# A three-part edit around float64 weights: the test for tiny values, the place of the rounding, and one normalisation step

## Chip, core and metric

The kernel runs on one core of one Trainium2 chip. The metric is the device time of one execution in microseconds (us); less is better. A core has a matrix engine (TensorE, PE in the profile, with its weight loads as PEld), a vector engine (VectorE, DVE), an activation engine (ScalarE, ACT), a general engine (GpSimd, POOL) and a queue engine (SyncE, SP) that issues the DMAs. Each engine works off its own instructions in a fixed order and waits on semaphores for the others.

## What is computed

```python
# 1. gated linear attention, B=4, H=8, S=768, D=48
state = f[t] * state + outer(k[t], v[t]);  y[t] = q[t] @ state
# 2. gated mixing branch (d_ff = 1024)
h = relu(x @ w_in);  u, v = h[..., :512], h[..., 512:]
v_n = (v - mean(v)) / sqrt(var(v) + 1e-6)
v_s = einsum('ts,bsd->btd', w_spatial, v_n) + b_spatial[None, :, None]
x = (u * v_s) @ w_out
# 3. token and channel layers (d_tok = 256, d_ch = 1536)
h = relu(x.T @ w_tok1) @ w_tok2;  u = x + h.T
out = u + relu(u @ w_ch1) @ w_ch2
```

Six weights (`w_in`, `w_out`, `w_t1`, `w_t2`, `w_c1`, `w_c2`) arrive as float64 and are read as pairs of 32-bit words; `w_sp` is float32.

## The kernel before, in words

The program is unrolled Python. A planner (the tile framework, with a time estimate of its own) sets each engine's order: it goes by the program's order where several instructions could go, and lets a later one go ahead when its data and its buffer are there. What the text writes as a place in the program is therefore a rank and not a time.

All float32 products are made of three products of rounded halves: a tile is split into a high part (`h`, fp32r) and a low part (`l`), and `mm3` (L158 to L164) issues high·high (L162), high·low (L163) and low·high (L164).

**Rounding of a weight piece.** `rounded` (L58 to L80) takes one piece of 128 rows by at most 384 columns: SP loads the raw words into `wst` (three buffers), DVE builds the exponent and sign (L66, L69), ACT scales the low word (L73), POOL adds the two (L74), ACT squares the high word (L75), and DVE (L79) sets to zero what is tiny, by comparing that square with `LEAST`. The result is in `wsa` (three buffers). `split_weight` (L101 on) makes the halves of a piece at once; `round_weight` (L82 on) stores rounded pieces in DRAM for later. There are 47 pieces: 9 of `w_in` and 4 of `w_out` go through `split_weight`, and 6 of `w_t1`, 4 of `w_t2`, 12 of `w_c1` and 12 of `w_c2` (the list `early`) through `round_weight`. `staged` runs a list of pieces as a pipeline of up to five steps, and `weave` spreads such lists evenly among the steps of a main list.

**Order of the stages.** Attention of the first half of batch 0 beside the pieces of `w_in`; then for each batch `s1` (two halves: `norm`, which is L424 to L445, makes v and its normalisation, `gate` makes u) and `s23` (`mix`: the product with `w_sp`, and `out1`: the product with `w_out`), with the attention of the next batch woven in. `norm` ends with L440 on DVE (`vf`, subtract the mean and multiply by `rs`), L444 on ACT (`vh`) and L445 on DVE (`vl`). The list `early` is woven in by `part`, in fifths: the mixing of batch 0, then `s1` of the second half and the mixing of batches 1 and 2. Then come the token layer (`c1`, `c2`) and the channel layer (`ff`), which runs over 4 batches by 2 halves by 12 blocks: `up1` is 9 matmuls into `p`, ACT makes `hh` (L641), DVE makes `hl` (L642), and `down` is 9 matmuls into three sums `po` (L654). For the next batch `c1` loads `xf` (L573) and ACT splits it (L576).

**The flag.** After the first pass `flag` says whether a decay product in `pend` was under `LOW`; if so, `body(True)` computes all again by a slower way. L550 to L556 make the flag. With the inputs here the second pass doesn't run.

Of the kernel before, what the change touches and what calls it, by code (L numbers as in the profile page):

```python
# [18 lines left out]
def tile_kernel(ctx, tc, fkqs, v, w_in, w_sp, b_sp, w_out, w_t1, w_t2, w_c1, w_c2, out):  # L19
    nc = tc.nc  # L20
# [34 lines left out]

    LEAST = 3.4332275390625e-05 ** 2

    def rounded(stage, a, src, c0, width, name):  # L58

# [14 lines left out]
        nc.gpsimd.tensor_tensor(out=a, in0=a, in1=lo, op=ALU.add)  # L74
        nc.scalar.activation(f32(hi), f32(hi), AF.Square)  # L75
        yield

        a = f32(a)
        nc.vector.scalar_tensor_tensor(out=a, in0=f32(hi), scalar=LEAST, in1=a, op0=ALU.is_ge, op1=ALU.mult)  # L79
        return a  # L80

    def round_weight(stage, src, name):  # L82

        if src.dtype != mybir.dt.uint64:
            return src, []
        rows, cols = src.shape
        dst = dram.tile([rows, cols], F32, name=name + "d")
        srcr = src.bitcast(U32).rearrange("(n p) c -> n p c", p=P)

        def piece(i, c0, width):  # L90
            at = stage.tile([P, WST], U32, tag="wsa", name=f"{name}da{i}{c0}")
            a = yield from rounded(stage, at[:, :width], srcr[i], c0, width, f"{name}d{i}{c0}")
# [8 lines left out]
    def split_weight(pool, stage, src, name, n, cols, eng, first=0, order=None, psum=None):  # L101

# [7 lines left out]
        def piece(i, c0, width):  # L110
# [3 lines left out]
            if wide:  # L114
                a = yield from rounded(stage, a, srcr[first + i], c0, width, f"{name}{i}{c0}")
                nc.scalar.copy(h[sl], a)
# [49 lines left out]
    def body(general):  # L166
# [248 lines left out]
        def s1(b, hf):  # L415
# [8 lines left out]
            def norm(i):  # L424
# [31 lines left out]
        def s23(b):  # L456
# [41 lines left out]
        winh, winl, steps = split_weight(  # L498
            wr, wst, w_in, "win", NK, DFF, nc.tensor, order=lambda x: sorted(x, key=lambda y: -y[1]), psum=ps_m
        )  # L500
# [3 lines left out]
        wsph, wspl, st_a = split_weight(wl, wst, w_sp, "wsp", NCH, S, nc.tensor, psum=ps_m)  # L504
        wouth, woutl, st_b = split_weight(wl, wst, w_out, "wout", NJ, DM, nc.tensor, psum=ps_m)
        s10, a01, sa = s1(0, 0), att(half(0, 1)), staged(st_a)
# [4 lines left out]
        early = []  # L511
        if not general:
            for name, src in (("wt1", w_t1), ("wt2", w_t2), ("wc1", w_c1), ("wc2", w_c2)):
                kept[name], x = round_weight(wst, src, name)
                early += x
            early = staged(early)
# [30 lines left out]

        if not general:
# [141 lines left out]
        op = e(tc.tile_pool(name="op", bufs=2))  # L690
        otp = e(tc.tile_pool(name="otp", bufs=3))
        c2h, c2l, st_c = split_weight(w3p, wst, kept["wc2"], "wc2", NF, DM, nc.vector)
# [68 lines left out]
```

## Time and profile before

| | |
|---|---|
| Time, median of 3 runs | 821.85 us (820.16 to 822.72) |
| The profiled execution | 819.0 us, of which its span (first to last instruction) is 817.2 us |
| PE busy | 777.3 us, 95% of the span |
| DVE, ACT, POOL busy | 420.3, 289.1, 211.1 us |
| Mean granted TensorE clock | 0.978 of full speed |
| DMA | 73.74 MB moved, 28% of the 16 engines' span |

How to read the rows further down: a row of a group of instructions gives line, engine, operation, what it writes and reads, the shapes, the count, then busy us and the mean ns of one, then the idle time before them and what ended it. A row of the chain of waits gives the shares of a stretch in the chain that ended last, by engine and line. PE's busy time is modelled from pipelined matmuls, so a PE that is busy all the time may still do less work than another.

### The profile page before, as it was taken

How to read it: one execution, taken by the hardware profiler on the slowest of the kernel's cores; microseconds unless marked ns; L12 is line 12 of the kernel's file. 1: busy time of each engine (PE TensorE's matmuls, PEld its weight loads, DVE VectorE, ACT ScalarE, POOL GpSimd, SP SyncE). 2: the span in 40 equal slices, each digit the busy share in tenths (PEclk: the TensorE clock that was granted, in tenths of full speed). 3: DMA queues.
4: the chain of work that ended last, by engine and by line, in shares of the span. 5: the costliest groups of instructions: out<-in, count | busy, mean ns of one | idle time of the engine just before them, and what ended most of it. 6: DMA issues, size and time to landing. Idle time of an engine off the chain costs nothing.

```text
span 817.2 us, 12758 instructions
## 1 busy us (share of the span) xinstructions
PE 777.3 (95%) x4860; PEld 716.3 (88%) x4860; DVE 420.3 (51%) x820; ACT 289.1 (35%) x649; POOL 211.1 (26%) x265
## 2 busy tenths in 40 slices
PE   5899899898989999999999999999999999999996
PEld 3577688688779888899899999999999999999995
DVE  6968599899898846673552532122122212221211
ACT  5766464555553444231632531122111211221110
POOL 4524344555641212110760330004000400010000
PEclk9899899999999999999999999999999999999998
DMA  7563435766474321220441410002000200000000
GB/s 254 176 207 104 147 96 164 236 225 214 146 237 140 101 96 59 65 67 24 128 126 40 138 56 30 1 4 85 1 30 0 87 1 30 1 8 24 30 1 33
DMA packets 39847, 73.74 MB, mean 90 GB/s; under 512 B 5216, under 2 KB 29664, under 8 KB 39776
## 3 DMA queue, kind: packets, MB, share of 16 engines
q1 hardware_dynamic: 39776, 72.83, 27.7%
q8 instruction: 40, 0.66, 0.3%
q14 instruction: 31, 0.25, 0.1%
HBM read 54.72 MB, written 15.73 MB: 86 GB/s over the span
## 4 chain that ended last, share of the span: by engine, by line
PE 71%; DVE 10%; DMA 10%; issue 4%; ACT 2%; SPq 1%; POOL 1%; DVEq 0%; ACTq 0%; POOLq 0%
PE po L654 19%; PE p L164 8%; PE p L162 8%; PE p L163 8%; DMA fkq<-in_fkq 3%; PE ps L162 3%; PE ps L164 3%; PE ps L163 3%; PE pa L259 2%; PE py L309 2%; PE py L315 2%; PE px L162 2%; PE px L163 1%; PE px L164 1%; DVE pg L236 1%
## 5 line engine op out<-in xcount | busy, mean ns | idle before, releaser
L642 DVE SCALAR_TENSOR_TENSOR hl<-p,hh 128x384 fp32r<-128x384 f32 x96 | 53.3, 557 | 188.4 <-ACT hh L641 188.4
L641 ACT ACTIVATE hh<-p 128x384 fp32r<-128x384 f32 x96 | 47.2, 492 | 198.0 <-PE p L164 198.0
L654 PE MATMUL po<-hl,wc2h 128*128 128x384 f32 x288 | 97.3, 338 | 0.0
L654 PE MATMUL po<-hh,wc2l 128*128 128x384 f32 x288 | 96.7, 336 | 0.0
L665 POOL TENSOR_TENSOR us<-uh,ul 128x384 f32<-128x384 f32 x24 | 24.3, 1024 | 232.0 <-DVE ul L625 214.7
L654 PE MATMUL po<-hh,wc2h 128*128 128x384 f32 x288 | 75.0, 336 | 0.0
L162 PE MATMUL ps<-wsph,vh 128*128 128x384 f32 x192 | 67.5, 351 | 0.0
L163 PE MATMUL ps<-wspl,vh 128*128 128x384 f32 x192 | 66.4, 346 | 0.0
L164 PE MATMUL ps<-wsph,vl 128*128 128x384 f32 x192 | 66.1, 346 | 0.0
L164 PE MATMUL p<-uh,wc1l 128*128 128x384 f32 x192 | 65.0, 338 | 0.0
L264 POOL TENSOR_SCALAR_AFFINE_SELECT am<-am 128x384 f32<-128x384 f32 x64 | 46.9, 748 | 69.7 <-ACT am L263 69.5
L163 PE MATMUL p<-ul,wc1h 128*128 128x384 f32 x192 | 64.7, 337 | 0.0
L162 PE MATMUL p<-uh,wc1h 128*128 128x384 f32 x192 | 64.2, 338 | 0.0
L654 PEld LDWEIGHTS po<-hl,wc2h 128*128 128x128 f32 x288 | 54.1, 188 | 0.1
L654 PEld LDWEIGHTS po<-hh,wc2l 128*128 128x128 f32 x288 | 54.1, 188 | 0.0
L654 PEld LDWEIGHTS po<-hh,wc2h 128*128 128x128 f32 x288 | 52.3, 188 | 0.0
L236 DVE TENSOR_TENSOR_SCAN pg<-fs,first 128x384 f32<-128x384 f32 x32 | 33.3, 1039 | 22.2 <-ACT first L379 22.1
L259 PE MATMUL pa<-fkq 48*128 48x128 f32 x384 | 40.6, 316 | 3.0 <-ACT am L263 3.0
L259 PEld LDWEIGHTS pa<-fkq 48*128 48x128 f32 x384 | 30.5, 204 | 12.3 <-issue 4.3
L162 PEld LDWEIGHTS ps<-wsph,vh 128*128 128x128 f32 x192 | 37.1, 193 | 2.4 <-issue 1.6
L625 DVE TENSOR_TENSOR ul<-p,uh 128x384 fp32r<-128x384 f32 x24 | 13.4, 557 | 47.6 <-ACT uh L624 47.6
L163 PEld LDWEIGHTS ps<-wspl,vh 128*128 128x128 f32 x192 | 37.0, 193 | 0.5 <-issue 0.2
(419 smaller groups left out, 1928.5 us busy)
## 6 DMA issues: line engine op xcount, KB each, us to landing
fkq<-in_fkq SPq DMA_DIRECT2D x31, 578.0 KB, 4.5
vt<-in_v SPq DMA_DIRECT2D x8, 576.0 KB, 5.9
x1d<-xs SPq DMA_DIRECT2D x24, 192.0 KB, 2.0
xf<-x1d SPq DMA_DIRECT2D x12, 384.0 KB, 4.5
out<-ot SPq DMA_DIRECT2D x24, 192.0 KB, 2.0
wspsa<-in_w_sp SPq DMA_DIRECT2D x12, 192.0 KB, 2.6
wc1d<-wc1da SPq DMA_DIRECT2D x12, 192.0 KB, 2.4
wc2d<-wc2da SPq DMA_DIRECT2D x12, 192.0 KB, 2.2
```

The lines of the kernel that those rows point to most:

```text
L162: nc.tensor.matmul(ps, lh, rh, start=first and i == 0, stop=False, **kw)
L163: nc.tensor.matmul(ps, lh, rl, start=False, stop=False, **kw)
L164: nc.tensor.matmul(ps, ll, rh, start=False, stop=i == n - 1, **kw)
L236: nc.vector.tensor_tensor_scan(out=pc, data0=fs[:, :W], data1=first, initial=0.0, op0=ALU.mult, op1=ALU.add)
L259: nc.tensor.matmul(pa[j][:, c, :], ki[64 * j : 64 * j + D, sl], qi[64 * j : 64 * j + D, sl], start=True, stop=True)
L264: nc.gpsimd.affine_select(out=am[j], in_=am[j], compare_op=ALU.is_ge, fill=0.0, base=0, pattern=[[0, NCW], [1, C]], channel_multiplier=-1,)
L309: nc.tensor.matmul(py[:112, c, :], now[c][:112, :112], qi[:112, c * C : (c + 1) * C], start=c == 0, stop=False, skip_group_check=True,)
L315: nc.tensor.matmul(py[64 * j : 64 * j + m, c, :], vt[:, c, h0 + D * j : h0 + D * j + m], am[j][:, c, :], start=False, stop=True, skip_grou ...
L641: nc.scalar.activation(hh, ps, AF.Relu)
L642: nc.vector.scalar_tensor_tensor(out=hl, in0=ps, scalar=0.0, in1=f32(hh), op0=ALU.max, op1=ALU.subtract)
L654: nc.tensor.matmul(po[c], l[:, ft, csl], r, start=ft == 0 and x == 0, stop=ft == NF - 1 and x == 2)
L665: nc.gpsimd.tensor_tensor(out=us[c], in0=f32(uh[:, c, tsl]), in1=f32(ul[:, c, tsl]), op=ALU.add)
```

## The change

There are three parts.

1. **The test for tiny values.** In the first pass the square (L75) and the comparison (L79) of all 47 pieces go away; the second pass keeps them. In their place `look` loads the raw words of all 47 pieces once more, during the channel layer of batches 0 to 2 (a pool `lkp` with two buffers), and DVE takes the smallest absolute high word of each row of a piece into a column of `lows`. `judge` scales `lows`, takes it together with `pend` and makes the flag, so a tiny weight now leads to the second pass. It stands in the channel layer of batch 3.
2. **The place of the rounding.** `early` is woven in by fourteenths: none in batch 0, 5 in batch 1 (`s1` of the second half, mixing), 7 in batch 2 (both halves of `s1`, mixing), 2 in `s1` of batch 3. The second pass rounds these weights itself.
3. **The normalisation.** `vf` is made by ACT as `r * rs + mr`, and DVE makes only the 128 by 1 `mr = -mean * rs`.

```diff
-    LEAST = 3.4332275390625e-05 ** 2
+    LEAST = 3.4332275390625e-05
+    NEAR = 3.5e-05
-    def rounded(stage, a, src, c0, width, name):
+    def rounded(stage, a, src, c0, width, name, tiny):
...
-        nc.scalar.activation(f32(hi), f32(hi), AF.Square)
+        if tiny:
+            nc.scalar.activation(f32(hi), f32(hi), AF.Square)
         yield
-        a = f32(a)
-        nc.vector.scalar_tensor_tensor(out=a, in0=f32(hi), scalar=LEAST, in1=a, op0=ALU.is_ge, op1=ALU.mult)
+        a = f32(a)
+        if tiny:
+            nc.vector.scalar_tensor_tensor(
+                out=a, in0=f32(hi), scalar=LEAST**2, in1=a, op0=ALU.is_ge, op1=ALU.mult
+            )
...
+    def look(stage):
+        def piece(n, src, c0, width):
+            st = stage.tile([P, WST, 2], U32, tag="look", name=f"look{n}")
+            nc.sync.dma_start(
+                out=st[:, :width, :].rearrange("p c t -> p (c t)"), in_=src[:, 2 * c0 : 2 * (c0 + width)]
+            )
+            yield
+            nc.vector.tensor_reduce(
+                out=lows[:, n : n + 1], in_=f32(st[:, :width, 1]), op=ALU.min, axis=mybir.AxisListType.X,
+                apply_absolute_value=True,
+            )
...
+                mr = smp.tile([P, 1], F32, tag="mr", name=f"mr{b}{hf}{i}")
                 nc.vector.tensor_scalar(
-                    out=vf, in0=r, scalar1=mv[:, 0:1], scalar2=rs, op0=ALU.subtract, op1=ALU.mult
-                )
+                    out=mr, in0=mv[:, 0:1], scalar1=rs, scalar2=-1.0, op0=ALU.mult, op1=ALU.mult
+                )
+                nc.scalar.activation(vf, r, AF.Identity, bias=mr, scale=rs)
...
-        part = lambda n: early[len(early) * n // 5 : len(early) * (n + 1) // 5]
+        part = lambda n, m: early[len(early) * n // 14 : len(early) * m // 14]
         for b in range(B - 1):
             if b:
-                weave(s1(b, 0), rest)
+                weave(s1(b, 0), rest, part(7 * b - 9, 7 * b - 7) if b > 1 else [])
...
-            weave(a, steps[:cut], out_steps if b == 0 else part(2 * b - 1))
-            weave(m, steps[cut:], part(2 * b))
+            weave(a, steps[:cut], out_steps if b == 0 else part(7 * b - 7, 7 * b - 5))
+            weave(m, steps[cut:], part(7 * b - 5, 7 * b - 2) if b else [])
...
-        weave(rest + s1(B - 1, 0) + s1(B - 1, 1), staged(st_a + st_b))
+        weave(rest + s1(B - 1, 0) + s1(B - 1, 1), staged(st_a + st_b), part(12, 14))
...
+        def judge():
+            nc.vector.tensor_scalar(
+                out=lows[:, :NLOW], in0=lows[:, :NLOW], scalar1=LOW / NEAR, scalar2=None, op0=ALU.mult
+            )
             nc.vector.tensor_reduce(
-                out=least, in_=pend.rearrange("p u c -> p (u c)"), op=ALU.min, axis=mybir.AxisListType.X
+                out=lows[:, NLOW : NLOW + 1], in_=pend.rearrange("p u c -> p (u c)"), op=ALU.min,
+                axis=mybir.AxisListType.X,
             )
+            nc.vector.tensor_reduce(out=least, in_=lows, op=ALU.min, axis=mybir.AxisListType.X)
...
+        looks = [] if general else staged(look(lkp))
+        part = lambda n: looks[len(looks) * n // (2 * B - 3) : len(looks) * (n + 1) // (2 * B - 3)]
         for b in range(B):
...
-                weave(ff(b, 0), ld, st_c[12:] if b == 0 else [])
+                weave(ff(b, 0), ld, st_c[12:] if b == 0 else part(2 * b - 1))
...
-                weave(ff(b, 0))
-            weave(ff(b, 1), more)
+                weave(ff(b, 0), [] if general else [judge])
+            weave(ff(b, 1), more, part(2 * b) if b + 1 < B else [])
```

## Rows read from the trace of the kernel before

**Rows 1.** The page's first part: busy us, share of the span, instructions.

```profile
PE 777.3 (95%) x4860; PEld 716.3 (88%) x4860; DVE 420.3 (51%) x820; ACT 289.1 (35%) x649; POOL 211.1 (26%) x265
```

**Rows 2.** Windows: stretch, length; busy (count) PE, PEld, DVE, ACT, POOL; clock; DMA; GB/s.

```profile
0.00:53.00 53.00, 38.48 (x273) 26.79 (x273) 43.61 (x84) 35.53 (x87) 22.28 (x44) 0.94 0.68 223
53.00:174.00 121.00, 112.01 (x761) 92.41 (x757) 97.79 (x206) 63.64 (x153) 51.95 (x63) 0.94 0.51 162
174.00:281.00 107.00, 100.16 (x679) 87.07 (x678) 95.19 (x190) 51.36 (x120) 45.82 (x54) 0.95 0.54 173
281.00:383.00 102.00, 102.00 (x727) 89.20 (x726) 60.59 (x129) 35.89 (x82) 16.35 (x35) 1.00 0.19 60
383.00:470.00 87.00, 85.62 (x483) 82.82 (x482) 41.55 (x70) 37.42 (x80) 38.74 (x43) 1.00 0.35 106
470.00:809.00 339.00, 339.00 (x1953) 338.05 (x1951) 80.62 (x144) 65.31 (x129) 35.93 (x28) 1.00 0.07 23
```

**Rows 3.** Chain of waits by line, windows 113:174, 174:281, 281:383, 470:817 in turn.

```profile
by line: DMA fkq<-in_fkq 17.1%; issue 12.7%; DMA wt1d30st<-in_w_t 7.2%; DMA wt2d1384st<-in_w_t 6.9%; DMA wc1d01152st<-in_w_c 6.1%; DMA wc1d0384st<-in_w_c 5.5%; DVE fkq L244 4.4%; SPq L93 2.4%; DVE wc1da L66 2.4%; DVE pg L241 2.3%; DVE vl L4
by line: issue 12.8%; PE ps L163 5.1%; PE ps L164 5.0%; DMA wc2d20st<-in_w_c 4.9%; PE ps L162 4.8%; DMA wc1d2768st<-in_w_c 4.5%; DVE wc2da L66 4.2%; DMA wc2d00st<-in_w_c 4.1%; DMA wc2d70st<-in_w_c 3.9%; DVE pg L236 3.6%; DVE wc2da L79 3.4%;
by line: PE ps L162 9.7%; PE ps L164 8.6%; PE pa L259 8.6%; PE ps L163 8.4%; PE py L315 6.2%; PE py L309 6.2%; PE px L162 5.8%; PE pu L162 4.7%; PE px L163 4.6%; PE pv L164 4.5%; PE px L164 4.4%; PE pv L162 4.4%; PE pu L164 4.1%; PE pu L163
by line: PE po L654 43.1%; PE p L164 17.7%; PE p L163 17.6%; PE p L162 17.6%; PE p L614 1.7%; DVE ot L675 0.2%; DVEq L710 0.1%; DVEq L675 0.0%
```

**Rows 4.** Windows of L79's instructions alone (DVE busy, count); then L75's sum.

```profile
0.00:53.00 53.00, 5.21 (x9) 0.94 0.68 223
53.00:174.00 121.00, 11.72 (x20) 0.94 0.51 162
174.00:281.00 107.00, 11.93 (x18) 0.95 0.54 173
...
sum 809.00, ACT 25.33; mean ACT 4.22
```

**Rows 5.** Groups by line: the normalisation, and the nearest operations.

```profile
L440 DVE TENSOR_SCALAR vf<-r,mv,rs 128x512 f32<-128x512 f32 x24 | 18.0, 750 | 9.7 <-POOL rs L438 9.6
L444 ACT CAST vh<-vf 128x512 fp32r<-128x512 f32 x24 | 14.9, 621 | 16.8 <-DVE vf L440 16.7
L576 ACT CAST x1h<-xf 128x768 fp32r<-128x768 f32 x12 | 10.0, 835 | 8.3 <-DMA xf<-x1d 8.1
L434 DVE BATCH_NORM_AGGREGATE mv<-bs 128x2 f32<-128x6 f32 x24 | 4.2, 175 | 0.3
```

**Rows 6.** The last rounding piece in time (start us, us), and the reduction of `pend`.

```profile
243.93 0.35 DVE L66 TENSOR_SCALAR wc2da<-wc2d110st 128x384 uint32<-128x384 uint32 x1
...
L550 DVE TENSOR_REDUCE least<-pend x1: 254/254/254, 360.2 to 360.2; 128x1 f32<-128x96 f32 x1
```

**Rows 7.** DMA issues: count, KB each, median us to landing.

```profile
xf<-x1d SPq DMA_DIRECT2D x12, 384.0 KB, 4.5
...
wout00st<-in_w_out SPq DMA_DIRECT2D x1, 384.0 KB, 3.1
...
wc2d30st<-in_w_c SPq DMA_DIRECT2D x1, 384.0 KB, 5.8
```

**Rows 8.** Waits (us in total, times, longest): ACT in 113:281, then window 470:809.

```profile
ACT wc2d20st L73 <- DMA wc2d20st<-in_w_c: 3.1, 1, 3.1
...
ACT x1h L576 <- DMA xf<-x1d: 6.0, 5, 2.1
```

**Rows 9.** Timeline in `ff`: start us, us, engine, line, what, [idle before].

```profile
487.31 0.49 ACT L641 ACTIVATE hh<-p 128x384 fp32r<-128x384 f32 x1 [2.67 <-PE p L164]
...
487.84 0.56 DVE L642 SCALAR_TENSOR_TENSOR hl<-p,hh 128x384 fp32r<-128x384 f32 x1 [2.61 <-ACT hh L641]
...
488.69 0.35 PE L654 MATMUL po<-hl,wc2h 128*128 128x384 f32 x1
488.87 0.34 PE L654 MATMUL po<-hh,wc2l 128*128 128x384 f32 x1
```

More of the change, by code (lines that the diff above doesn't have):

```diff
@@ L74, in rounded, with round_weight @@
         nc.gpsimd.tensor_tensor(out=a, in0=a, in1=lo, op=ALU.add)
-        nc.scalar.activation(f32(hi), f32(hi), AF.Square)
+        if tiny:
+            nc.scalar.activation(f32(hi), f32(hi), AF.Square)
         yield
         a = f32(a)
-        nc.vector.scalar_tensor_tensor(out=a, in0=f32(hi), scalar=LEAST, in1=a, op0=ALU.is_ge, op1=ALU.mult)
+        if tiny:
+            nc.vector.scalar_tensor_tensor(
+                out=a, in0=f32(hi), scalar=LEAST**2, in1=a, op0=ALU.is_ge, op1=ALU.mult
+            )
         return a
-    def round_weight(stage, src, name):
+    def round_weight(stage, src, name, tiny):
         if src.dtype != mybir.dt.uint64:
@@ L91, in piece @@
             at = stage.tile([P, WST], U32, tag="wsa", name=f"{name}da{i}{c0}")
-            a = yield from rounded(stage, at[:, :width], srcr[i], c0, width, f"{name}d{i}{c0}")
+            a = yield from rounded(stage, at[:, :width], srcr[i], c0, width, f"{name}d{i}{c0}", tiny)
             nc.sync.dma_start(out=dst[i * P : (i + 1) * P, c0 : c0 + width], in_=a)
@@ L99, in tile_kernel, with split_weight @@
     kept = {}
-    def split_weight(pool, stage, src, name, n, cols, eng, first=0, order=None, psum=None):
+    wides = [w for w in (w_in, w_out, w_t1, w_t2, w_c1, w_c2) if w.dtype == mybir.dt.uint64]
+    NLOW = sum(w.shape[0] // P * -(-w.shape[1] // WST) for w in wides)
+    lows = const.tile([P, NLOW + 1], F32, name="lows")
+    def look(stage):
[9 more added lines that the diff above has]
+            )
+        out = []
+        for w in wides:
+            wr = w.bitcast(U32).rearrange("(n p) c -> n p c", p=P)
+            for i in range(w.shape[0] // P):
+                for c0 in range(0, w.shape[1], WST):
+                    out.append(partial(piece, len(out), wr[i], c0, min(WST, w.shape[1] - c0)))
+        assert len(out) == NLOW
+        return out
+    def split_weight(pool, stage, src, name, n, cols, eng, first=0, order=None, psum=None, tiny=False):
         wide = src.dtype == mybir.dt.uint64
@@ L114, in piece @@
             if wide:
-                a = yield from rounded(stage, a, srcr[first + i], c0, width, f"{name}{i}{c0}")
+                a = yield from rounded(stage, a, srcr[first + i], c0, width, f"{name}{i}{c0}", tiny)
                 nc.scalar.copy(h[sl], a)
@@ L498, in body @@
         winh, winl, steps = split_weight(
-            wr, wst, w_in, "win", NK, DFF, nc.tensor, order=lambda x: sorted(x, key=lambda y: -y[1]), psum=ps_m
+            wr, wst, w_in, "win", NK, DFF, nc.tensor, order=lambda x: sorted(x, key=lambda y: -y[1]), psum=ps_m,
+            tiny=general,
         )
@@ L504, in body @@
         wsph, wspl, st_a = split_weight(wl, wst, w_sp, "wsp", NCH, S, nc.tensor, psum=ps_m)
-        wouth, woutl, st_b = split_weight(wl, wst, w_out, "wout", NJ, DM, nc.tensor, psum=ps_m)
+        wouth, woutl, st_b = split_weight(wl, wst, w_out, "wout", NJ, DM, nc.tensor, psum=ps_m, tiny=general)
         s10, a01, sa = s1(0, 0), att(half(0, 1)), staged(st_a)
@@ L511, in body @@
         early = []
[L512 to L516, printed above, removed]
-        part = lambda n: early[len(early) * n // 5 : len(early) * (n + 1) // 5]
+        for name, src in (("wt1", w_t1), ("wt2", w_t2), ("wc1", w_c1), ("wc2", w_c2)):
+            kept[name], x = round_weight(wst, src, f"{name}{int(general)}", general)
+            early += x
+        early = staged(early)
+        part = lambda n, m: early[len(early) * n // 14 : len(early) * m // 14]
         for b in range(B - 1):
             if b:
-                weave(s1(b, 0), rest)
+                weave(s1(b, 0), rest, part(7 * b - 9, 7 * b - 7) if b > 1 else [])
             a, rest = s1(b, 1), []
@@ L546, in body @@
         h1p = wr2.enter_context(tc.tile_pool(name="h1p", bufs=1, side="right"))
-        if not general:
+        def judge():
+            nc.vector.tensor_scalar(
+                out=lows[:, :NLOW], in0=lows[:, :NLOW], scalar1=LOW / NEAR, scalar2=None, op0=ALU.mult
+            )
             nc.vector.tensor_reduce(
-                out=least, in_=pend.rearrange("p u c -> p (u c)"), op=ALU.min, axis=mybir.AxisListType.X
+                out=lows[:, NLOW : NLOW + 1], in_=pend.rearrange("p u c -> p (u c)"), op=ALU.min,
+                axis=mybir.AxisListType.X,
             )
+            nc.vector.tensor_reduce(out=least, in_=lows, op=ALU.min, axis=mybir.AxisListType.X)
             row = ps_s.tile([P, W], F32, tag="s", name="row")[:1, :P]
@@ L691, in body @@
         otp = e(tc.tile_pool(name="otp", bufs=3))
+        lkp = e(tc.tile_pool(name="lkp", bufs=2))
         c2h, c2l, st_c = split_weight(w3p, wst, kept["wc2"], "wc2", NF, DM, nc.vector)
```

## The prediction, made before the changed kernel was run

> **What bounds the kernel now.** First the page's busy line: PE is busy 95% of the span, DVE 51%, ACT 35% [rows 1]. So time can be won only where PE idles or is slowed, and the mean says nothing on where. Next a table by stage [rows 2], with edges where the first normalisation of a batch starts (batch 0 at 53 us, 1 at 174, 2 at 281, 3 at 383; the channel layer from about 470). The reader is to see two halves. From 281 us on PE is busy without a break, but for 1.4 us, and its clock is full: nothing that DVE or ACT save there is worth anything. Before 281 PE idles 14.5, 9.0 and 6.8 us in the three stages, its clock is 0.94 to 0.95, and DVE is busy 82%, 81% and 89%. Then the chain of waits for four stretches [rows 3]: after 281 it is nearly all PE; before, it runs through loads of weight pieces, loads of `fkq` and DVE's steps of the rounding. So the first 281 us are bound by DVE and by the rounding's own chain as much as by PE, and the rest by PE alone.
>
> Stages 174 to 281 and 281 to 383 do the same main work (one batch of `s1` and `s23`, eight attention units), and only the first has rounding: the last of its 47 pieces is begun at 243.9 us [rows 6]. It takes 107 us against 102. The later stage even issues 48 matmuls more (727 against 679) [rows 2]; at the 0.18 us between two matmul starts [rows 9] these are 8.6 us of work. So rounding and the DVE load cost the stage 5 + 8.6, some 13 us, and that is all it can give back.
>
> **Part 1a, L75 and L79 go.** L79 takes 5.2, 11.7 and 11.9 us of DVE in the three stages (9, 20 and 18 pieces), L75 25.3 us of ACT in all [rows 4]. Each piece also loses two steps of its chain, and its `wst` buffer is free earlier, so SP issues the next load sooner.
>
> **Part 3, the normalisation.** DVE loses L440 at 0.75 us and gains a 128 by 1 operation, priced like L434 at 0.175 [rows 5]. This is 0.57 us a time, with 6 in each stage from 53 us on: 3.4 us each. ACT gains `vf`. The trace has no ACT pass with two per-row operands; the bounds are L444, as wide, at 0.62 us, and L576, half as wide again, at 0.84 [rows 5]. I take 0.8, since the two operands must cost something, so 24 x 0.8 = 19 us, less than the 25.3 that L75 frees: ACT ends 6 us lighter. The wait of ACT for DVE, now before `vf` and no longer before `vh`, has the same work queued behind it on ACT (`hh`-like copies, `fs`, `am`), and it ends 0.57 us sooner; then ACT is held 0.8 us longer. In the stages after 281 I cost it at nothing: PE hides it, and if that cover is gone it is 12 x (0.8 + 0.175 - 0.75) = 2.7 us.
>
> **What 1a and 3 give, by stage.** *174 to 281*: DVE falls by 11.9 + 3.4 = 15.3 us, from 95.2 to 79.9, which is 75% of 107. The stage without rounding has 59% (60.6 of 102) [rows 2]. The relief closes 14 of the 30 points, about half, so I take half of the 13 us: **6 us**. Bounds: 0 and 13. *53 to 174*: DVE falls by 11.7 + 3.4 = 15.1 us, from 81% to 68%. What can be won is PE's idle 9.0 us and what the low clock costs: a mean of 0.94 between the levels 0.5 and 1 is 12% of 121 us at half speed, 14.5 us, at most 7.3 us lost; 16 us together. But 17% of the chain there is loads of `fkq` [rows 3], which the change leaves alone; I take a third: **5 us**, bounds 0 and 16. *0 to 53*: the relief is 5.2 us of DVE; the first loads and the chain of the first attention units stay. I take **2 us**, bounds 0 and 5.
>
> **Part 2, the later place.** A place is a rank to the planner, and the trace shows how little it binds: the last piece stands in the mixing of batch 2, after 281 us, and ran at 243.9; the reduction of `pend` stands behind the mixing of batch 3 and ran at 360.2 [rows 6]. The pieces ran ahead of their places as soon as a buffer was free. I expect the same after: every instruction of a piece (its load and its store on SP, L66 and L69 on DVE, L73 on ACT, L74 on POOL) gets a lower rank but is still issued early, on SP ahead of `fkq` loads that stand later, as now. So I take **0**. If the rank does bind, up to 24 of the 38 steps of `early` move behind 281, and the two stages before get DVE, ACT and the DMAs to themselves. That is worth at most what is left of their 13 and 16 us, 18 us; the stages behind have PE full and DVE at 59% and 48% as cover, and without it could lose what 174 to 281 lost before, 13 us. Bounds: -18 and +13.
>
> **Part 1b, the looks.** 47 loads of 384 KB (nine of 256) and 47 DVE reductions come into the channel layer, where PE is full. One reduction is 128 by 384; L550 took 0.25 us for 96 elements and L434 0.175 for 6 [rows 5, 6], so 0.9 ns an element and some 0.51 us, 23 us in all, beside 80.6 us of DVE work in 339 [rows 2]. They will run soon after 470, as fast as two buffers allow, not where they are woven in. The danger is the order on DVE: behind a reduction that waits for its load stands `hl` (L642), and PE's next-but-few matmul waits for that. `hl` ended at 488.40 and was used at 488.69: 0.29 us of slack; DVE idles 2.6 us of each 3.2 [rows 9]. Landed in time, a reduction fits the gap, and a chance overlap costs under (0.51 - 0.29)^2 / 2 / 3.2 us, nothing. Landed late by t, it has 2.6 - 0.5 = 2.1 us of room at most. Loads of this size took 3.1 us (quiet) to 5.8 (busy), `xf` 4.5 [rows 7]; the planner's order was wrong by 1.2 us on the mean for `xf` in this very stage (6.0 us in 5 waits), and by up to 3.1 us for a weight piece [rows 8]. With t = 1.2 and the room spread evenly from 0 to 2.1, a look costs 0.91^2 / 2 / 2.1 = 0.2 us, 47 make 9 us. Those waits are the late ones of 12 `xf` loads, and looks come one at a time, so I take a third: **+3 us**. Bounds: 0 and 47 x (1.2 - 0.29) = 43 us. `out` stores and `xf` loads queue behind looks on SP; the first have the next half to drain, the second are used tens of us later: 0.
>
> `judge` adds two DVE operations of 0.25 us; its one PE transpose waits for them, at most 0.8 us once, and it ends half a batch before the end: 0, in the rounding of the above.
>
> **The sum.** -2 - 5 - 6 + 3 = -10 us against the profiled execution's 819.0, of which 817.2 is the span and 1.8 lies around it. The median of the runs is 821.85, 2.85 above that one; I put the change on the median: **812 us**.
>
> **The rivals.**
> *The looks hold DVE* (ends slower). Two buffers in flight make a loop: load, reduction, next load. If on the chip that loop is slower than in the planner's estimate, DVE's order makes `hl` go at the loop's pace, and each look costs PE the difference. For: the 0.29 us of slack, the waits for `xf`. Against: the DMA share there is 0.07, and a lone load took 3.1 us. At half of the upper bound, 21 us, less the 13 us won before: 830 us. It decides from 13 / 47 = 0.28 us of PE per look on. The Trainium skill ("Perfetto Trace Analysis", section "Tensor Engine Instruction (MATMUL, LD_WEIGHTS)") states that DVE, unlike PE's weight loads, takes its queue strictly in order; the waits of ACT for `xf` in front of `hh` look the same, and it would be this rival's 830.
> *DVE was not what held PE* (no change). Then weight loads, 17% of the chain in 174 to 281 (wc2d20, wc1d2768, wc2d00, wc2d70) [rows 3], still set the pace; the gain shrinks to 3 us and the looks take it back: 822 us.
> *The rank binds*: of the 13 and 16 us most is won, say 22 in place of 11: 801 us.
> *ACT becomes the bound of the normalisation.* All 24 chains get longer by 0.8 + 0.175 - 0.75 = 0.225 us; on the path throughout that is 5 us: 817 us. For: ACT waited 16.7 us for L440 [rows 5]. Against: ACT is busy 48% from 174 to 281 [rows 2]. The Trainium skill ("ScalarE: Activation LUTs", section "Rules for kernel authors") says that adds and multiplies belong on VectorE, which would speak against part 3 and give this 817; its section "What ACT_TABLE_LOAD costs" prices the pass at 0.80 us (an estimate: 186 ns + 0.833 ns x 512 + 93 ns for each per-row operand), which leaves the sum at 812.
>
> **How the numbers follow.** Forecast 0.50, looks hold DVE 0.18, no change 0.15, rank binds 0.12, ACT 0.05. About 0.3% (2.5 us, 819.4 to 824.3) is what a measurement of this kernel can tell from no change. The forecast, with its own range of 805 to 820, is faster in nine tenths of its cases (0.45); with the rank (0.12), ACT (0.04) and a few of the looks' cases (0.02) faster gets 0.63. No change (0.11) and edges of the others give same 0.17, slower 0.20. The range leaves out a tenth at either end: below, half of the rank's cases and the best of the forecast, 798; above, half of the looks' cases, 830.
>
> **What would show it.** *Right*: the stage of batch 1 (174 to 281 now) shorter by about 6 us with DVE near 75%, that of batch 0 by 5; L66 of the pieces still between 70 and 240 us; PE without a break in the channel layer, and DVE's waits for the looks' loads small. *Wrong*: DVE waiting for `look` loads by tens of us with `hl` late behind it, PE idle after 470; pieces spread to 400 us (part 2 was undervalued); DVE far below 75% before 281 with PE's idle time unchanged (DVE was not the bound); ACT idle in front of `vf`, with `vh` and the mixing late.

## The result, and the profile after

The changed kernel takes 831.3 us (median of 4 runs, 828.9 to 835.5) against 821.0 us for the kernel before in the same comparison: 1.0142 times as long, with a 95% interval of 1.0107 to 1.0177. It is slower by 1.4%, where 812 us, faster, was predicted; 831.3 also lies above the range. The rival "the looks hold DVE" had put 830 us.

Where did the time go? I cut both profiled executions at the same points of the work: the first matmul of each batch's `pv` (the product that makes v), the first transpose of `c2`, the first and last `po` matmul, and the matmuls at a quarter and at half of `po`. All lengths are in us.

| stretch | before | after | difference |
|---|---|---|---|
| start, to `pv` of batch 0 | 53.2 | 52.9 | -0.3 |
| batch 0 | 121.0 | 121.0 | 0.0 |
| batch 1 | 106.5 | 101.5 | -5.0 |
| batch 2 | 102.5 | 102.8 | +0.3 |
| batch 3 and `c1`, to the first transpose of `c2` | 70.3 | 70.1 | -0.2 |
| `c2`, to the first `po` | 13.0 | 16.9 | +3.9 |
| channel layer, first quarter | 90.8 | 109.1 | +18.3 |
| channel layer, second quarter | 90.4 | 90.0 | -0.4 |
| channel layer, second half | 161.0 | 160.4 | -0.6 |
| from the last `po` to the end | 8.5 | 6.8 | -1.7 |
| span | 817.2 | 831.5 | +14.3 |

So 5 us were won in batch 1 and 22 us lost in one place, from `c2` to the end of the first quarter of the channel layer. The changed file's lines have moved; the ones that matter here are the look's load (L114) and reduction (L118), `mr` (L472), `vf` on ACT (L475), `hh` and `hl` (L679, L680) and `po` (L692).

The page's busy line of the changed kernel:

```profile
PE 783.2 (94%) x4860; PEld 713.4 (86%) x4860; DVE 409.4 (49%) x822; ACT 285.3 (34%) x626; POOL 206.4 (25%) x265
```

DVE and ACT got lighter, as meant (420.3 and 289.1 us before, [rows 1]), and yet the span grew. So the sums say nothing; the stages do. These are the windows of the changed kernel by stage, with the columns of [rows 2]:

```profile
53.00:174.00 121.00, 112.30 (x757) 91.05 (x758) 91.41 (x191) 59.84 (x139) 52.97 (x66) 0.97 0.56 174
174.00:275.00 101.00, 96.87 (x673) 83.28 (x672) 75.75 (x160) 46.35 (x105) 35.96 (x50) 0.98 0.51 162
275.00:378.00 103.00, 103.00 (x729) 90.61 (x728) 56.78 (x129) 40.21 (x88) 17.15 (x35) 1.00 0.19 60
378.00:465.00 87.00, 82.66 (x462) 79.33 (x460) 39.58 (x69) 38.61 (x80) 40.76 (x43) 1.00 0.40 122
465.00:560.00 95.00, 83.72 (x441) 78.24 (x442) 44.38 (x84) 18.73 (x39) 10.82 (x8) 0.96 0.65 189
560.00:823.00 263.00, 263.00 (x1523) 262.38 (x1522) 60.58 (x112) 49.59 (x98) 25.77 (x21) 1.00 0.07 23
```

The second row is what was hoped for: DVE at 75.75 of 101 us, PE idle 4 us. The fifth is the loss: PE idle 11.3 us, a granted clock of 0.96 and 441 matmuls, in a stretch that was full before. The sixth is full again. DVE is busy only 47% of the fifth stretch, so it isn't short of time; it waits, and the chain of waits from 470 to 560 us names for what:

```profile
by line: DMA look<-in_w_c 48.1%; DMA look<-in_w_t 15.9%; DVE lows L118 11.5%; DMA look<-in_w_in 8.0%; PE po L692 3.6%; DMA look<-in_w_out 3.5%; DVE wc2l L157 2.8%; issue 2.7%; PE p L193 1.5%; PE p L194 1.5%; PE p L195 1.4%; DVE hl L680 1.0%
```

Three quarters are loads of looks and 11.5% their reductions. The timeline shows one turn of the loop (start us, us, engine, line, what, idle before it and for what):

```profile
499.87 0.49 ACT L679 ACTIVATE hh<-p 128x384 fp32r<-128x384 f32 x1 [3.10 <-PE p L195]
...
502.86 0.55 DVE L118 TENSOR_REDUCE lows<-look 128x1 f32<-128x384 f32 x1 [0.97 <-DMA look<-in_w_t]
...
505.01 0.55 DVE L118 TENSOR_REDUCE lows<-look 128x1 f32<-128x384 f32 x1 [1.60 <-DMA look<-in_w_c]
505.48 0.55 DVE L680 SCALAR_TENSOR_TENSOR hl<-p,hh 128x384 fp32r<-128x384 f32 x1
506.08 0.19 PEld L692 LDWEIGHTS po<-hl,wc2h 128*128 128x128 f32 x1 [1.05 <-DVE hl L680]
506.09 0.45 PE L692 MATMUL po<-hl,wc2h 128*128 128x384 f32 x1 [0.73 <-DVE hl L680]
```

Which `hh` belongs to which `hl`, and which `hl` to which matmul? The text's `step(n)` issues `up1` of block n and then `down` of block n-1, and each trace has 96 `hh`, 96 `hl` and 96 groups of three `po<-hl` matmuls, so they are matched by counting. The `hl` of 505.48 belongs to the `hh` that ended at 500.36 and could have started then. But two reductions of looks stood ahead of it on DVE and waited 0.97 and 1.60 us for their loads; `hl` came at 505.48, and PE stood still for 0.73 us. The Trainium skill ("Perfetto Trace Analysis", section "Tensor Engine Instruction (MATMUL, LD_WEIGHTS)") states that DVE takes its queue strictly in order; the trace agrees, since DVE was idle for both of these waits while `hl` was ready.

How early did PE have `hl` before the change? The prediction read 0.29 us, from the `hl` that ended at 488.40 to the matmul at 488.69 [rows 9]. By the count that matmul reads the `hl` of the block before, and the one of 488.40 is used only from 491.68 on. The kernel before:

```profile
484.67 0.56 DVE L642 SCALAR_TENSOR_TENSOR hl<-p,hh 128x384 fp32r<-128x384 f32 x1 [2.61 <-ACT hh L641]
...
491.68 0.19 PEld L654 LDWEIGHTS po<-hl,wc2h 128*128 128x128 f32 x1
```

So `hl` led its user by 3.28 us, a whole block. In blocks 7 to 24, which make up most of the first quarter, the lead was never under 3.07 us before; in the changed kernel it was 0.05 us in 12 of these 18 blocks, with PE waiting, and 3 us again when the looks were over.

The waits from 465 to 560 us (us in total, times, longest) and the group of the reductions over the whole span:

```profile
DVE lows L118 <- DMA look<-in_w_c: 30.1, 24, 2.2
DVE lows L118 <- DMA look<-in_w_t: 10.4, 10, 1.6
PEld po L692 <- DVE hl L680: 13.0, 13, 2.1
PE po L692 <- DVE hl L680: 8.7, 10, 1.8
...
L118 DVE TENSOR_REDUCE lows<-look 128x1 f32<-128x384 f32 (+1 forms) x47 | 24.7, 526 | 50.6 <-DMA look<-in_w_c 30.1 <-DMA look<-in_w_t 10.4 <-DMA look<-in_w_in 7.4
```

DVE waited 50.6 us for 47 loads, 1.08 us each, and PE waited 8.7 us for `hl`, where it waited 0.0 us in the kernel before.

### The profile page after: what moved, and what is told of

It reads as the page before. It is cut to its first block, busy times and chain, and to the rows that moved or that the text cites. A ratio compares the mean times of both kernels' runs of the same rounds, so it can differ in the third digit from the quotient of the medians.

```text
span 831.5 us, 12770 instructions
## 1 busy us (share of the span) xinstructions
PE 783.2 (94%) x4860; PEld 713.4 (86%) x4860; DVE 409.4 (49%) x822; ACT 285.3 (34%) x626; POOL 206.4 (25%) x265
## 4 chain that ended last, share of the span: by engine, by line
PE 56%; DMA 17%; DVE 5%; POOL 2%; SPq 2%; issue 1%; ACT 1%; DVEq 0%; POOLq 0%; ACTq 0%
PE po L692 15%; PE p L195 6%; PE p L194 6%; PE p L193 6%; DMA look<-in_w_c 5%; PE ps L193 3%; PE ps L195 3%; PE ps L194 3%; DMA look<-in_w_in 3%; PE pa L290 2%; DMA look<-in_w_t 2%; PE px L193 1%; DVE lows L118 1%; PE px L195 1%; PE px L194 1%
## 5 line engine op out<-in xcount | busy, mean ns | idle before, releaser
L680 DVE SCALAR_TENSOR_TENSOR hl<-p,hh 128x384 fp32r<-128x384 f32 x96 | 53.2, 555 | 158.5 <-ACT hh L679 158.4
L679 ACT ACTIVATE hh<-p 128x384 fp32r<-128x384 f32 x96 | 47.1, 492 | 198.6 <-PE p L195 198.6
L692 PE MATMUL po<-hl,wc2h 128*128 128x384 f32 x288 | 99.1, 344 | 8.7 <-DVE hl L680 8.7
L692 PE MATMUL po<-hh,wc2l 128*128 128x384 f32 x288 | 97.9, 340 | 0.0
L692 PE MATMUL po<-hh,wc2h 128*128 128x384 f32 x288 | 76.9, 343 | 4.0 <-ACT hh L679 2.5
L692 PEld LDWEIGHTS po<-hl,wc2h 128*128 128x128 f32 x288 | 54.6, 190 | 13.1 <-DVE hl L680 13.0
L295 POOL TENSOR_SCALAR_AFFINE_SELECT am<-am 128x384 f32<-128x384 f32 x64 | 40.1, 636 | 97.0 <-ACT am L294 96.9
L692 PEld LDWEIGHTS po<-hh,wc2h 128*128 128x128 f32 x288 | 53.3, 190 | 5.1 <-ACT hh L679 4.3
L692 PEld LDWEIGHTS po<-hh,wc2l 128*128 128x128 f32 x288 | 54.8, 190 | 0.0
L118 DVE TENSOR_REDUCE lows<-look 128x1 f32<-128x384 f32 (+1 forms) x47 | 24.7, 526 | 50.6 <-DMA look<-in_w_c 30.1
L267 DVE TENSOR_TENSOR_SCAN pg<-fs,first 128x384 f32<-128x384 f32 x32 | 31.5, 985 | 36.2 <-ACT first L410 36.2
L290 PE MATMUL pa<-fkq 48*128 48x128 f32 x384 | 43.8, 313 | 0.0
L290 PEld LDWEIGHTS pa<-fkq 48*128 48x128 f32 x384 | 32.2, 200 | 11.3 <-issue 6.1
L340 PE MATMUL py<-fkq,state 112*112 112x128 f32 x160 | 33.1, 299 | 6.0 <-DVE state L315 3.8
```

The costliest lines, as they stand in the source:

```text
L118: nc.vector.tensor_reduce(out=lows[:, n : n + 1], in_=f32(st[:, :width, 1]), op=ALU.min, axis=mybir.AxisListType.X, apply_absolute_value=True,
L267: nc.vector.tensor_tensor_scan(out=pc, data0=fs[:, :W], data1=first, initial=0.0, op0=ALU.mult, op1=ALU.add)
L290: nc.tensor.matmul(pa[j][:, c, :], ki[64 * j : 64 * j + D, sl], qi[64 * j : 64 * j + D, sl], start=True, stop=True)
L295: nc.gpsimd.affine_select(out=am[j], in_=am[j], compare_op=ALU.is_ge, fill=0.0, base=0, pattern=[[0, NCW], [1, C]], channel_multiplier=-1,)
L340: nc.tensor.matmul(py[:112, c, :], now[c][:112, :112], qi[:112, c * C : (c + 1) * C], start=c == 0, stop=False, skip_group_check=True,)
L679: nc.scalar.activation(hh, ps, AF.Relu)
```

## The experiments

The theory: the looks run early and as a closed loop of two buffers (load, reduction, next load). The planner had put them in DVE's order at the pace that it reckons for this loop; on the chip the loop is slower, and since `hl` stands in between, PE goes at the loop's pace once the lead of `hl` is used up. That the loop is closed is seen in the trace: from the 12th look on each reduction begins 0.02 us after its load has landed, and the load that takes over its buffer is issued 0.03 us after its end. The pace planned can be read from PE: between the reductions at 502.86 and 553.63 us there are 24 looks and 220 matmuls. At 0.173 us a matmul (549 in 94.7 us where PE is undisturbed) these are 38.0 us of work, 1.58 us a look; they took 50.77 us, 2.12 us a look. The excess is 0.53 us a look, 12.8 us in this stretch, in 9.1 of which PE was idle; its granted clock there was 0.97. Rivals: the traffic of the loads slows what else moves; the reductions' own time on DVE is too much; the loss has nothing to do with the looks.

**No looks.** The changed kernel without loads and reductions; `lows` is filled with ones, so tiny weights are not tested for.

```diff
-        looks = [] if general else staged(look(lkp))
+        looks = []
+        if not general:
+            nc.gpsimd.memset(lows, 1.0)
```

> The changed kernel without the 47 looks (their loads and reductions are left out, the column block that they fill is set to 1.0; so the test for tiny weights isn't made). All theories that blame the looks: the channel layer runs at PE's pace as before, about 17 us come back, 812 to 816 us. If the looks are not the cause (a change of order before 465 us is), it stays at 828 to 832 us.

Measured: 813.8 us, 0.9917 of before (0.9884 to 0.9950); first quarter of the channel layer 90.4 us, `c2` 13.0. By the ratios (1.0142 and 0.9917) the looks cost 18 us, and by the cuts of the profiles 22, all of it in that place; the rest of the change is worth -6.8 us.

**Loads only.** The 47 loads stay, the reductions go.

```diff
-            nc.vector.tensor_reduce(
-                out=lows[:, n : n + 1], in_=f32(st[:, :width, 1]), op=ALU.min, axis=mybir.AxisListType.X,
-                apply_absolute_value=True,
-            )
...
+        if not general:
+            nc.gpsimd.memset(lows, 1.0)
```

> The 47 loads stay, nothing reads them (the reductions are left out). Loop theory (DVE stands before a reduction whose load is late, with hl behind it): no wait on DVE, so as without looks, 812 to 817 us. Theory of DMA traffic (17 MB more slow PE, stores or other loads): 826 to 832 us. Theory of DVE's own time: 812 to 817 us.

Measured: 815.8 us, 0.9949 (0.9917 to 0.9980); first quarter 91.3 us, but `c2` 15.3, so 2 of the 4 us lost in `c2` may be the loads' own. Beyond that the traffic is not the cause: the window from 465 to 560 us moves even more per second (197 GB/s) and PE is full.

```profile
465.00:560.00 95.00, 94.73 (x549) 94.18 (x548) 26.43 (x44) 22.91 (x44) 17.74 (x13) 1.00 0.65 197
```

**Reductions only.** One tile stays resident, filled with ones by POOL; the 47 reductions read it, and there are no loads.

```diff
-            st = stage.tile([P, WST, 2], U32, tag="look", name=f"look{n}")
-            nc.sync.dma_start(
-                out=st[:, :width, :].rearrange("p c t -> p (c t)"), in_=src[:, 2 * c0 : 2 * (c0 + width)]
-            )
+            if n == 0:
+                kept["look"] = st = stage.tile([P, WST, 2], U32, tag="look", name="look")
+                nc.gpsimd.memset(f32(st.rearrange("p c t -> p (c t)")), 1.0)
+            st = kept["look"]
```

> The 47 reductions stay, all of one tile that is filled once, with no load to wait for (the loads are left out). Loop theory: 25 us of DVE work fit beside hl, 812 to 818 us. Theory of DVE's own time (a reduction in front of hl uses up its slack of 0.29 us): 824 to 832 us. DMA theory: 812 to 817 us.

Measured: 830.9 us, 1.0120 (1.0073 to 1.0168): the loop theory's expectation missed. But the loss lies elsewhere: `c2` took 22.5 us instead of 13.0 and the first quarter 97.0. Without loads nothing held the reductions back, and the planner put all of them into one stretch, 457 to 486 us, in runs of up to 14, ahead of `wc2l` and `ul`, which the transition to the channel layer needs. The chain of waits from 448 to 500 us says so:

```profile
by line: DVE lows L118 22.3%; PE po L692 17.1%; PE p L195 10.2%; PE p L194 10.1%; PE p L193 9.7%; DMA xf<-x1d 6.6%; DVE wc2l L157 5.5%; issue 3.3%; PE px L195 2.7%; DVE ul L663 2.7%; PE px L193 2.3%; PE px L194 2.3%; PE p L652 2.3%; ACT x1h
```

No load of a look is in it. So this run has a cause of its own, or DVE's time is the cause in both. The run after "paced" below was made to tell these apart.

**Paced.** Loads and reductions as in the change, but each reduction may go on DVE only behind the `hl` that the text puts before it, so that the looks are spread over the half batches in which they are written.

```diff
-            nc.vector.tensor_reduce(
+            with tc.issue_after(kept["hl"].ins):
+                nc.vector.tensor_reduce(
...
-                nc.vector.scalar_tensor_tensor(
+                kept["hl"] = nc.vector.scalar_tensor_tensor(
```

> All 47 loads and reductions, but each reduction is queued on DVE behind the hl that stands before it in the program, so that the looks spread over batches 0 to 2 and a load has about two blocks of the channel layer (some 6 us) to land. Loop theory: the load has landed when DVE comes to its reduction, 812 to 818 us, faster than the kernel before. DVE's own time or DMA traffic: 824 to 832 us as before, since both amounts are unchanged.

Measured: 816.9 us, 0.9952 of before (0.9927 to 0.9976); `c2` 13.1, first quarter 91.8, second 90.1. The same loads, reductions and buffers, without the loss. DVE's waits for looks from 465 to 650 us are now two, of 0.8 and 0.5 us:

```profile
DVE lows L119 <- DMA look<-in_w_c: 0.8, 1, 0.8
...
DVE lows L119 <- DMA look<-in_w_out: 0.5, 1, 0.5
```

**Reductions in the channel layer.** As "reductions only", but held behind the first `hl`.

```diff
+            with tc.issue_after(kept["hl"].ins):
+                nc.vector.tensor_reduce(
...
+                kept["hl"] = kept["hl"] or x
```

> The changed kernel without the 47 loads; 47 reductions of one resident tile, queued on DVE behind the first low part of the channel layer, so that none stands in the stage before it. It tells what made the reductions without loads lose 16 us. If it was the burst in front of the work that the second token layer and the first blocks need: 0 to 2 us lost, 813 to 817 us, the second token layer back at 13 us and the first quarter of the channel layer at 91. If DVE's time behind the slack of the low part is itself the cause: about 0.3 us of PE for each reduction, 825 to 830 us, with the first quarter of the channel layer at 100 us or more.

Measured: 818.6 us, 1.0003 (0.9971 to 1.0035); `c2` 13.0, first quarter 94.3. Between the two expectations, nearer to the burst: 3.5 us are left of the 15.7 that "reductions only" lost in `c2` and the first quarter. And these 3.5 us aren't DVE's time behind `hl`. The windows of the two stretches in which the 47 reductions stand (464 to 492 us):

```profile
464.00:476.00 12.00, 10.11 (x47) 9.53 (x47) 12.00 (x27) 6.28 (x12) 7.94 (x5) 0.86 0.55 172
476.00:494.00 18.00, 18.00 (x105) 18.00 (x105) 17.22 (x38) 3.36 (x7) 0.00 (x0) 1.00 0.00 1
```

All the loss is in the first, where the reductions stand among `wc2l` and `ul` and PE's waits are for the halves of `xf`; what makes these late there is not shown. In the second DVE is busy 96% of the time, and PE has no break. So the reductions' time costs PE nothing where the order leaves `hl` its lead. Against the run without looks the ratio to before is higher by 0.0086, 7 us; each of the two ratios is known to some 3 us, so how much more than 3.5 us is real stays open.

**Four buffers.** The changed kernel with four buffers for the looks.

```diff
-        lkp = e(tc.tile_pool(name="lkp", bufs=2))
+        lkp = e(tc.tile_pool(name="lkp", bufs=4))
```

> The changed kernel with four buffers in place of two for the looks. Loop theory: with four loads under way both the planner's loop and the chip's are bound by the DMAs' rate; a lone load moves 384 KB in about 1.5 us of transfer, so the chip's pace drops from 2.1 to about 1.6 us a look, while the planner crowds them closer as well; if the planner's pace falls in step the loss stays near 17 us (828 to 833 us), if the loop's latency was all, it falls under 8 us (816 to 822 us). Theory of DVE's own time: unchanged, 828 to 833 us.

Measured: 814.3 us, 0.9971 (0.9936 to 1.0005); first quarter 92.9 us. Better than both expectations. The looks run as early as in the change (their reductions from 455 to 518 us), and 2 us are lost in the first quarter: PE waited for `hl` once, 2.0 us, at the first block. From 471.90 to 517.70 us there are 37 looks, one each 1.24 us, and PE has no break, so the PE work between two is as long: no excess. The lead of `hl` is never under 0.59 us after the first block.

```profile
471.90:517.70 45.80, 45.80 (x264) 45.76 (x264) 29.32 (x60) 9.31 (x19) 1.79 (x1) 1.00 0.91 308
```

DVE's waits for looks in all fell from 50.6 to 17.7 us.

**One buffer.** The same with `bufs=1`.

> The changed kernel with one buffer for the looks in place of two: a load is issued only when the reduction of the look before it has ended. Loop theory (the loads' and reductions' loop takes longer on the chip than the planner reckons, and DVE's fixed order hands the difference to the high and low parts and so to PE): the loop is then a whole latency longer and so is the difference, from some 0.5 us a look to about 1.0 us, so 40 to 50 us are lost in the channel layer against 18 to 22, and the time is 850 to 860 us. DVE's time alone as the cause: the same 47 reductions, so the time stays near 831 us. Traffic of the loads as the cause: fewer loads at a time, so the same or less than 831 us.

Measured: 837.3 us, 1.0239 (1.0181 to 1.0296). The direction is the loop theory's, and DVE's time as the cause falls, for the reductions are the same; but the loss is 26 us (`c2` +2.0, first quarter +17.7, second +5.9), not 40 to 50. From 478.65 to 555.39 us there are 22 looks:

```profile
478.65:555.39 76.74, 67.85 (x368) 63.76 (x367) 23.31 (x49) 10.75 (x22) 3.04 (x3) 0.98 0.37 109
```

3.49 us a look, and 368 x 0.173 / 22 = 2.89 us of PE work between two: 0.60 us excess, against 0.53 with two buffers. My expectation took the excess to double, since with two buffers two loads share it. They don't: a load alone in flight lands sooner. The loads of `in_w_c` in the changed kernel, with one buffer and with four (count, KB each, median us to landing):

```profile
look<-in_w_c SPq DMA_DIRECT2D x24, 384.0 KB, 3.5
```

```profile
look<-in_w_c SPq DMA_DIRECT2D x24, 384.0 KB, 3.1
```

```profile
look<-in_w_c SPq DMA_DIRECT2D x24, 384.0 KB, 4.3
```

So more buffers make each load slower and the loop faster. By (load + reduction) / buffers, with 0.55 us for the reduction, a turn is 3.65, 2.03 and 1.21 us with one, two and four buffers; measured were 3.49 (where a third of the looks move only 256 KB), 2.12 and 1.24. Also to be seen: with one buffer DVE waits 102 us for looks, twice as long as with two, and PE loses about as much. Most of that wait was in the plan (2.89 us of PE work to a look) and lay beside other work:

```profile
DVE hl L680 <- ACT hh L679: 117.8, 58, 5.4
DVE lows L118 <- DMA look<-in_w_c: 58.5, 24, 3.2
...
DVE lows L118 <- DMA look<-in_w_t: 23.0, 10, 3.0
DVE lows L118 <- DMA look<-in_w_in: 10.3, 7, 3.3
DVE lows L118 <- DMA look<-in_w_out: 10.3, 4, 2.7
```

**Paced, four buffers.** Both edits together.

> The changed kernel with each look's reduction held behind the low part that the text puts before it, and four buffers for the looks in place of two. Loop theory: the looks, held to their places, leave their loads enough time already with two buffers, so no gain from four: 815 to 817 us, as with two. If waits of DVE for loads still cost something there: 812 to 814 us.

Measured: 817.4 us, 0.9969 (0.9938 to 0.9999); first quarter 91.1 us (`c2` 15.0). No gain over either alone: once the excess is gone, a second cure buys nothing.

**The other parts alone**, each put into the kernel before. First the test taken out (lines L75 and L79) with nothing in its place, so tiny weights are not handled:

```diff
-        nc.scalar.activation(f32(hi), f32(hi), AF.Square)
...
-        nc.vector.scalar_tensor_tensor(out=a, in0=f32(hi), scalar=LEAST, in1=a, op0=ALU.is_ge, op1=ALU.mult)
```

> The kernel before without L75 and L79 (the test for tiny weights is left out), all else as before. By the prediction's stage sums the relief of DVE and the shorter chain of a piece give 2 + 4 + 4.5 us, so 810 to 813 us. Rival: the changed kernel won only 5 us before the channel layer, all of it in the stage of batch 1; then this gives 815 to 819 us, and the stage of batch 0 (53 to 174 us) stays at 121 us because more pieces move into it.

Measured: 818.3 us, 0.9982 (0.9947 to 1.0018): not told from no change, and not the 810 to 813 us of the prediction's sums. In its profile batch 1 was shorter, 102.7 us, and so was batch 0, 115.7 us, which the rival kept at 121; but the start was longer, 57.0 us, so that the first 174.3 us of the kernel before became 172.7.

Then the normalisation alone (its diff stands in the change above):

> The kernel before with vf made on ScalarE and nothing else. By the prediction's sums DVE loses 3.4 us in each of two stages that it holds up: 1 to 3 us won, 818 to 820 us. Rival (the normalisation's chain gets longer by 0.225 us, 24 times, on the path): 2 to 5 us lost, 823 to 827 us.

Measured: 815.6 us, 0.9953 (0.9927 to 0.9978), some 3.9 us faster, a little more than the 1 to 3 expected; batch 1 104.2 us. `vf` on ACT takes 814 ns:

```profile
L444 ACT ACTIVATE vf<-r,mr,rs 128x512 f32<-128x512 f32 x24 | 19.4, 814 | 9.0 <-DVE mr L441 8.6
```

Then the later place alone (the `part` lines of the change):

> The kernel before with the list of later weights woven in by fourteenths from batch 1 on, and nothing else. Rank theory (a place is a rank; pieces run as soon as a buffer is free): L66 of the pieces still between 70 and 250 us but for the last few, time within 3 us of the kernel before. Rival (the place binds): pieces up to 400 us, stages of batch 0 and 1 shorter by up to 18 us together.

Measured: 819.0 us, 1.0003 (0.9979 to 1.0027): nothing. All but two of the pieces were begun by 242.0 us, as before; the last two, which the text puts in batch 3, went at 390.3 and 397.8 us.

Last, the paced kernel with the earlier places:

```diff
-        part = lambda n, m: early[len(early) * n // 14 : len(early) * m // 14]
+        part = lambda n: early[len(early) * n // 5 : len(early) * (n + 1) // 5]
```

> The changed kernel with the looks held as before, and the rounding of the later weights put back at its earlier places. By the run of the later place alone (no change) it should be the same as with the later place, 815 to 818 us. If the later place moves pieces into the stage of batch 0 and so eats up there what the test's leaving gives: the stage of batch 0 falls from 121 to 116 us, that of batch 1 is longer by less, and the time is 812 to 815 us.

Measured: 817.1 us, 0.9977 (0.9951 to 1.0003), batch 0 121.0 us. The place is worth nothing beside the other parts either, and it isn't what kept batch 0 at 121 us: 24 pieces were begun in it with either place.

## Why the prediction was wrong

The step that failed is **Part 1b, the looks**. It had the place (a late load in front of `hl`) and the early start right, and the cost of a look wrong: +3 us for all, where `c2` and the first quarter lost 22. It reckoned the looks as single late events against a slack of `hl`; the runs showed a closed loop that is 0.53 us a turn slower than the order allows for. "Paced", "four buffers" and "loads only" each take away one link of the loop, and each brings the first quarter back to 91 to 93 us.

- *"0.29 us of slack"* was misread: the lead of `hl` was 3.28 us. With it the prediction's own sum, a load 1.2 us late and at most 2.1 us of room, gives no loss at all. That it foresaw any loss is luck, and so is the nearness of the rival's 830 us to 831.3, since its 21 us are half of a bound made with the 0.29.
- *"Late by t = 1.2 with the room spread evenly from 0 to 2.1: 0.2 us a look"* treated each look as a chance event in a schedule that otherwise stands. In a closed loop the lateness adds up: the order on DVE has `hl` and looks side by side at the planned pace of 1.58 us, a late look delays `hl`, and the next load is issued only after the late reduction. At 0.53 us a turn six or seven turns use up 3.28 us (an estimate from these two numbers), and from then on the whole excess reaches PE in each turn.
- *"Looks come one at a time, so I take a third"* was against the same paragraph, which had them run as fast as two buffers allow. At that pace 384 KB every 2.1 us is a stream (0.65 of the DMA engines), and a load in it took 3.5 us, not the 3.1 of a quiet one [rows 7].
- The number was at hand. The loop is (load + reduction) / 2: by the prediction's own rows (3.1 + 0.5) / 2 = 1.8 us at best and (5.8 + 0.5) / 2 = 3.15 us at worst. And loads that come 1.2 us later than the planner reckons [rows 8] make a turn of two buffers 1.2 / 2 = 0.6 us longer than planned, near the 0.53 measured. The rival weighed the same loop, and its point of decision, 0.28 us a look, was passed by nearly a factor of two. It got 0.18; with a planner seen to be late by 1.2 us on the mean it deserved the larger chance. "Against: the DMA share there is 0.07" counted the traffic before the change, not the looks' own.

The other steps:

- *The reduction itself*, 0.51 us by estimate: 0.553 for 384 elements. Right.
- *Batch 1, -6 with DVE near 75%*: -5.0, and 75.75 / 101 = 75%. Right, and it holds in every profile: the changed kernel and the nine runs that alter it have 100.8 to 102.3 us there, the kernel before 106.5 and with the later place alone 105.8.
- *Batch 0, -5*: 0.0. Not seen, and the cause is not settled. One pair of profiles is a weak reading: in the changed kernel and the eight runs that alter only its looks, batch 0 took 117.9 to 123.6 us, 120.8 on the mean. DVE fell only from 97.8 to 91.4 us there, not by 15, partly because 24 pieces instead of 21 were begun in it. With the earlier places it was the same (24 pieces, 92.1 us of DVE, 121.0 us), so that run doesn't tell what a lighter DVE would give. The chain of waits of the changed kernel from 53 to 174 us runs through loads, as 17% of it in the second half already did before [rows 3]:

```profile
by line: DMA vt<-in_v 5.5%; DMA fkq<-in_fkq 4.4%; DMA wc10d2384st<-in_w_c 3.9%; DMA wc10d0384st<-in_w_c 3.5%; DMA wc10d2768st<-in_w_c 3.5%; DMA wc10d10st<-in_w_c 3.1%; SPq L427 3.1%; issue 3.0%; DMA wt20d00st<-in_w_t 2.3%; POOL wc10da L75 2
```

  That loads bind this stage is read from this row alone; no run took them away.
- *The start, -2*: -0.3, but one profile can't tell (see the last section).
- *Part 2, 0*: right, alone and together, pieces ahead of their places as told. The rival "the rank binds" falls.
- *Part 3, by its share of DVE's relief (3.4 of 15.3 and of 15.1 us) some 2.5 us of the gain*: -3.9 alone, known to some 2 us. `vf` was taken at 0.8 and measured 0.815, `mr` at 0.175 and measured 0.213. The rival "ACT becomes the bound" falls, since the normalisation alone made the kernel faster; ACT's wait in front of `vf` is 9.0 us, less than the 16.7 in front of `vh` before [rows 5]:

```profile
L475 ACT ACTIVATE vf<-r,mr,rs 128x512 f32<-128x512 f32 x24 | 19.6, 815 | 9.4 <-DVE mr L472 9.0 <-DVE mv L465 0.2
```

  The Trainium skill's rule that adds and multiplies belong on VectorE ("ScalarE: Activation LUTs", section "Rules for kernel authors") went the wrong way in this kernel, where DVE was the fuller engine in the stages with rounding; the page's estimate of the pass, 0.80 us, agrees with the 0.815 of the row.
- *Parts 1a, 2 and 3 together, -13*: -6.8 us without the looks. About half, and a little more than the three alone add up to (-1.5, -3.9 and +0.2, each known to 2 or 3 us). What fell short most is part 1a: -1.5 alone, where its share of the sum is some 10.5.
- *`judge`, 0*: right; the stretch after the last `po` didn't get longer (8.5 and 6.8 us).

So of the 22 us that the looks cost by the cuts (18 by the ratios) 3 were foreseen, and of the 13 that the rest should give 7 came. A kernel that keeps the change and mends the looks beats the changed one by 14 us and more. Paced, 0.9952, also beats the kernel before; four buffers, 0.9971 (0.9936 to 1.0005), can't be told from it, nor from paced.

## What to carry to other kernels

A load with few buffers and a consumer in an in-order engine's queue is a loop with a pace of its own, (load + consumer) / buffers. Compare that pace with the one at which the program has put the consumers between the critical work: if it is slower, the difference adds up turn by turn, uses up any lead, and then the critical engine pays all of it in each turn, however idle the engine in between. A lead only puts this off. (And when a lead is read from a trace, match the producer with its own consumer by counting: the next use in time can belong to the block before.) The cure is to space the consumers or to have more buffers, and either is enough; work that is out of its place by nobody's order, as the burst of reductions showed, can cost nearly as much as the wait.

## What else the runs showed

- **A wait is not a loss.** With one buffer DVE waited 102 us for looks and the kernel lost 26 us; with two, 50.6 and 22. Only the part above the plan reaches PE, and that only when the lead of `hl` is gone.
- **Double-buffering was too little.** The Trainium skill ("Trainium Kernel Development and Optimization", section "Best Practices") advises to double-buffer so that DMA overlaps compute. Here two buffers cost 14 us against four (1.0142 and 0.9971 of before).
- **The start varies by some 5 us, with the granted clock.** From 30 to 40 us, the kernel without looks ran at a clock of 0.59 in its profiled execution and the paced one at 1.00:

```profile
30.00:40.00 10.00, 8.24 (x36) 4.86 (x36) 9.67 (x18) 7.67 (x20) 5.60 (x7) 0.59 0.61 197
```

```profile
30.00:40.00 10.00, 8.23 (x64) 5.27 (x64) 9.56 (x17) 7.78 (x20) 5.43 (x6) 1.00 0.62 201
```

  In the same ten microseconds PE did 36 matmuls in the one and 64 in the other; batch 0 began at 57.8 and 52.0 us. In the 14 profiles it began at 57.0 to 57.8 us in the four whose mean clock up to there was 0.88, and at 51.5 to 54.2 in the ten with 0.94 or more. A mean of 0.59 is a stretch mostly at the lower level, 1.2 GHz. In both PE had been mostly idle from 28 to 32 us (1.5 and 2.0 us of work in 4). In 79 runs of the kernel before the mean clock lay between 0.972 and 0.992, and the time fell by 3.4 us for each 0.01 of it (correlation -0.59). A difference of 2 us at the start of two single profiles is therefore no reading at all; medians of several runs are.
